# First chunk of an mLSTM cell: gate a spread by TensorE in bfloat16 parts, exponentials four heads at a time, front steps in a new order

## The chip, the cores and the metric

One core of a Trainium2 chip. The time is microseconds on the device for one execution, median of several. The engines are TensorE (PE; its weight loads are listed apart as PEld), VectorE (DVE), ScalarE (ACT), GpSimd (POOL) and SyncE (SP), which here only issues DMAs.

## The reference

Two parts: a recurrent cell with exponential gates over 4 batches x 8 heads, 768 steps, 40 columns a head, then a GELU layer with two weight matrices that arrive in float64.

```python
for t in range(S):
    m_new = np.maximum(f_gate[:, :, t] + m, i_gate[:, :, t])
    f_stab = np.exp(f_gate[:, :, t] + m - m_new)
    i_stab = np.exp(i_gate[:, :, t] - m_new)
    m = m_new
    C = f_stab * C + i_stab * outer(vt, kt)
    n = f_stab * n + i_stab * kt
    h_tilde = C @ qt
    denom = max(abs(n . qt), 1.0)
    y[:, :, t] = sigmoid(o_gate[:, :, t]) * h_tilde / denom
x = y.transpose(0, 2, 1, 3).reshape(B * S, H * D)     # 3072 x 320
h = x @ w_in                                          # 320 x 2048
out = (0.5 * h * (1 + erf(h / sqrt(2)))) @ w_out      # 2048 x 320
```

## The kernel before

The 768 steps are cut into 6 chunks of 128. In a chunk the recurrence becomes products: with bl the running sum of f, a = i - bl and M the running maximum of a, step s contributes to step t with the weight W[s, t] = exp(a[s] - M[t]) for s <= t and 0 beyond. Scores k.q are multiplied by W, and times v (with a column of ones for the denominator) give the new part; the state kept in `state` gives the older one. After the cell of a chunk its 512 tokens (4 batches x 128) go through the up product, GELU and the down product. Work of the next chunk's cell is laced into the down product of the one before.

The order is written by hand: every engine runs its instructions in the order in which the program issues them. `FRONT` is the order for everything up to the down product of chunk 0: a string of words, each a letter with a batch or a count. `play` (L1125) walks it.

- Weights: `P` (`fetch`, L358) starts the DMA of one piece of w_in or w_out as 32-bit words; `K` (`conv_one`, L370) does three VectorE and two ScalarE instructions of its conversion to float32, `J` (`conv_two`, L388) the last two VectorE instructions, and then starts the fetch of the piece four further on (`fetch(i + NB)`; four buffers `bits`). Pieces 0 to 9 are w_in, 10 to 25 w_out. An up step needs pieces 0, 1 and 2, the second 3 and 4 too, and so on; row f of the down product needs piece 10 + f.
- Loads on SP's queue: `L` q and k of a batch, `O` v and o, `B` the M of a later chunk spread over the 128 partitions (512 KB from `M_d`). The batches are counted on over the chunks: `L4` is batch 0 of chunk 1.
- Gates: before the string, `gates_of(0, 1)` makes bl, a and M of chunk 0 on 32 rows (one a head and batch). `E` does chunk 1, `N` chunks 2 to 5, `Q` and `D` turn their decays by TensorE, `d` and `q` spread the last of them (`pd`).
- Cell of chunk 0, in small letters: `w` weights, `g` sigmoid of o, `t` turn k and q (8 transposes into `ps_tr`, copied by ScalarE), `s` scores (two banks of `ps_mm`, tag a, then VectorE's product with W, L550), `c` carry (vw, 8 matmuls, state), `v` values (16 matmuls), `y` finish (6 VectorE instructions), `x` turn y (3 transposes, copied to `first_x`). Cell of chunk 1, in capitals, likewise, with `M` the masking by GpSimd and `R` the split of x.
- `A` and `U` are up steps (L814, L820, then GELU L824) for the first and second half of the tokens, `F` rows of the down product (L1052); rows need all four banks of `ps_mm`. `Z` splits a weight of the next up product.
- Fillers, whose results nobody reads: `k` n runs n matmuls (L228), and `I` n puts n of them (L408) ahead of the next bank's first use.

Weights of chunk 0 (L452): M of that chunk is cut into three bfloat16 parts that add up to it exactly (L307 to L314). For four heads a bank `pm` takes four matmuls that spread the row M of a head over all partitions (the stationary operand is a column of `row`, an identity, repeated 128 times), and one that adds 1e30 where s > t. ScalarE then takes exp(a - pm) head by head, with a, turned to the partitions (`aT`, L315), as bias. In the later chunks M comes by DMA, and the exponentials are head by head too.

Of the kernel before, what the change touches and what calls it, by code (L numbers as in the profile page):

```python
# [9 lines left out]
F32 = mybir.dt.float32  # L10
F32R = mybir.dt.float32r
BF16 = mybir.dt.bfloat16
U32 = mybir.dt.uint32
AF = mybir.ActivationFunctionType
OP = mybir.AluOpType

P = 128
# [8 lines left out]


FRONT = """
    I2 O0 g0 L0 P0 L1 E k1 t0 P1 P2 w0 k7 N k2 w1 O1 K L2 Q s0 O3 w2 q D
    k2 d P3 t1 w3 c0 L3 J v0 t2 K K y0 s1 I7 v1 I8 O2 J g1 L4 I5 c1 K I1  # L30
    I2 y1 s2 x0 t3 B4 O4 B5 g2 J x1 s3 v2 c2 L5 y2 H T0 x2 G0 v3 g3 c3 K y3
    M1 J L6 J A x3 M0 K W0 O7 K A O6 O5 J M2 W1 S0 C0 K J J T1 U U
    K L7 V0 K T2 r J J A G2 K G1 Y0 W2 S1 K M3 C1 A J S2 J K W3 K
    V1 C2 Y1 T3 J J U U S3 V2 K K J G3 J Y2 C3 X0 K V3 J K F J F
    K K B8 F J K F F J K F F F R0 X1 J J K F J F K X2 F J
    K F J Y3 K F R1 e J F Z B9 B10 F X3 R2 Z R3 F p"""
DOWN = """
    M0 F Z F L3 W0 M1 Z W1 S0 C0 F F h0 Q2 F K2 G1 D3 B3 Z V0 G2 M2 W2 M3 W3 V1 K3 Q3 F G0 S2 Z Y0 G3 C2 h2 F
    F Y1 X0 V2 V3 F N F j R0 Y2 Y3 X1 F F X2 R1 F R2 X3 R3 F"""
# [3 lines left out]
def kernel(  # L43
# [16 lines left out]
    nc = tc.nc  # L60

    B, H, S, D = q.shape
    L = P
    NCH = S // L
# [3 lines left out]
    BH = B * H  # L68
# [21 lines left out]
    ps_mm = ctx.enter_context(tc.tile_pool(name="ps_mm", bufs=2, space=bass.MemoryType.PSUM))  # L90
    gp = ctx.enter_context(tc.tile_pool(name="gp", bufs=1))
    gate_ctx = ExitStack()
    gates = gate_ctx.enter_context(tc.tile_pool(name="gates", bufs=1))
# [6 lines left out]
    ident = const.tile([P, P], F32, name="ident")  # L100
# [3 lines left out]
    aT = const.tile([P, NCH, BH], F32, name="aT")  # L104
# [10 lines left out]
    W = {n: shared([P, H, L], F32, f"W{n}") for n in range(B - 1)}  # L115
# [7 lines left out]
    eye = gates.tile([P, P], BF16, name="eye")  # L123
    beyond = gates.tile([P, L], BF16, name="beyond")
# [55 lines left out]
    def load_M(n, to=None):  # L180

        if not B <= n < NCH * B:
            return
        c, b = divmod(n, B)
        src = M_d[c - 1, b * H:(b + 1) * H, :]
        if to is not None:
            Mb[n] = to
            nc.sync.dma_start(out=to, in_=src.unsqueeze(0).to_broadcast([P, H, L]))
            return
        Mb[n] = shared([P, H, L], F32, "W") if n // 2 == NW else wts.tile([P, H, L], F32, name="W", tag="W")  # L190
        nc.sync.dma_start(out=Mb[n].rearrange("p h l -> p (h l)"),
                      in_=src.rearrange("h l -> (h l)").unsqueeze(0).to_broadcast([P, H * L]))
# [17 lines left out]

    keep = gates.tile([BH, NCH, L], F32, name="keep")
    bl = gates.tile([BH, NCH, L], F32, name="bl")
    a = gates.tile([BH, NCH, L], F32, name="a")
    M = gates.tile([BH, NCH, L], F32, name="M")
    ew = gates.tile([BH, NCH - 1, L], F32, name="ew")
    gg = gates.tile([BH, NCH - 1, L], F32, name="gg")
    m0 = gates.tile([BH, NCH], F32, name="m0")
    M_left = gg[:, 0:2]
    M_parts = gates.tile([3 * BH, L], BF16, name="M_parts")
    row = gates.tile([3 * BH, BH], BF16, name="row")  # L220
    for j in range(3):
        m = slice(BH * j, BH * (j + 1))
        nc.scalar.copy(out=row[m], in_=ident[m, m])

    def warm(n):
        cold = ps_h.tile([P, P], F32, name="cold", tag="h")
        for _ in range(n):
            nc.tensor.matmul(cold, w_out[:, 0, 0:P], w_out[:, 0, 0:P], start=True, stop=True, skip_group_check=True)  # L228
# [20 lines left out]
    def gates_turned(*parts):  # L249

        for src, dst in parts:
            n = dst.shape[1]
            pg = ps_tr.tile([P, n, BH], F32, name="pg", tag="tr")
            for c in range(n):
                nc.tensor.transpose(pg[:, c, :], src[:, c, :], ident[0:BH, 0:BH])
            nc.vector.tensor_copy(out=dst, in_=pg)
# [13 lines left out]
    def gates_of(c0, c1):  # L270

        flat = lambda t: t[:, c0:c1].rearrange("p c l -> p (c l)")
        nc.vector.tensor_tensor_scan(out=flat(bl), data0=flat(keep), data1=flat(f_sb), initial=0.0,
                                     op0=OP.mult, op1=OP.add)
        nc.vector.tensor_tensor(out=a[:, c0:c1], in0=i_sb[:, c0:c1], in1=bl[:, c0:c1], op=OP.subtract)
        for c in range(c0, c1):
            nc.vector.tensor_tensor_scan(out=M[:, c], data0=a[:, c], data1=a[:, c], initial=m0[:, c:c + 1],
                                         op0=OP.max, op1=OP.max)
            if c + 1 < NCH:
                nc.vector.tensor_tensor(out=m0[:, c + 1:c + 2], in0=bl[:, c, L - 1:L], in1=M[:, c, L - 1:L],  # L280
                                        op=OP.add)

    def decays_of(e0, e1, g0, g1):

        e, g = slice(e0, e1), slice(g0, g1)
        nc.vector.tensor_tensor(out=ew[:, e], in0=a[:, e], in1=M[:, e, L - 1:L].to_broadcast([BH, e1 - e0, L]),
                                op=OP.subtract)
        nc.vector.tensor_tensor(out=gg[:, g], in0=m0[:, g0 + 1:g1 + 1].unsqueeze(2).to_broadcast([BH, g1 - g0, L]),
                                in1=M[:, g0 + 1:g1 + 1], op=OP.subtract)
        nc.scalar.activation(out=ew[:, e], in_=ew[:, e], func=AF.Exp)  # L290
# [6 lines left out]
    def decays_last(g0, g1):  # L297
        g = slice(g0, g1)
        pd = ps_tr.tile([P, g1 - g0, BH], F32, name="pd", tag="tr")
        nc.tensor.matmul(pd.rearrange("p c n -> p (c n)"), last, gT[:, g].rearrange("p c n -> p (c n)"),  # L300
                         start=True, stop=True)
        by_half = pd.rearrange("p c (n two) -> p c n two", two=2)
        for hip in range(2):
            nc.vector.tensor_copy(out=dec[halves[hip], g], in_=by_half[halves[hip], :, :, hip])


    gates_of(0, 1)  # L307
    left = M[:, 0]
    for j in range(3):
        part = M_parts[BH * j:BH * (j + 1)]  # L310
        nc.vector.tensor_copy(out=part, in_=left)
        if j < 2:
            nc.vector.tensor_tensor(out=M_left[:, j], in0=left, in1=part, op=OP.subtract)
            left = M_left[:, j]  # L314
    gates_turned((a[:, 0:1], aT[:, 0:1]))  # L315
    warm(6)

    def second_gates():
        gates_of(1, 2)
        nc.sync.dma_start(out=M_d[0], in_=M[:, 1])  # L320
        gates_turned((a[:, 1:2], aT[:, 1:2]))
# [84 lines left out]
    def unread(bank):  # L406
        for _ in range(idle[0]):
            nc.tensor.matmul(bank, ident, ident, start=True, stop=True, skip_group_check=True)  # L408
        idle[0] = 0
# [25 lines left out]
    class Cell:  # L435
# [16 lines left out]
        def weights(self, b):  # L452

            n = self.c * B + b
            if self.c > 0:
                W[n] = M_n = Mb.pop(n)
            elif n not in W:
                W[n] = wts.tile([P, H, L], F32, name="W", tag="W")
            for h in range(H):
                r = b * H + h  # L460
                if self.c > 0:
                    src = M_n[:, h, :]
                else:


                    if h % 4 == 0:
                        pm = ps_mm.tile([P, 4, L], F32, name="pm", tag="b")
                        unread(pm[:, 0, :])
                        for j in range(4):
                            nc.tensor.matmul(pm[:, j, :], row[:, r + j:r + j + 1].to_broadcast([3 * BH, P]), M_parts,  # L470
                                             start=(j == 0), stop=False, skip_group_check=True)
                        nc.tensor.matmul(pm, eye, beyond.unsqueeze(1).to_broadcast([P, 4, L]), start=False, stop=True,
                                         skip_group_check=True)
                    src = pm[:, h % 4, :]
                nc.scalar.activation(out=W[n][:, h, :], in_=src, func=AF.Exp, scale=-1.0, bias=aT[:, self.c, r:r + 1])  # L475
            if n in (B, B + 1):
                load_M(n + 2)

# [653 lines left out]
    def in_turn(steps):  # L1132
        todo = list(steps)
        return lambda: todo.pop(0)() if todo else None
# [9 lines left out]
    def first_blocks():  # L1144

        copy_chunk(2, range(1))
        for r in (32, 96):
# [7 lines left out]
                 d=lambda: decays_last(0, 1), q=lambda: decays_last(1, NCH - 1), r=halves_out, p=halves_back,  # L1155
                 A=in_turn(first_up_steps(0)), U=in_turn(first_up_steps(1)), e=first_blocks, F=in_turn(first_down_steps(first_g)),
                 K=in_turn(lambda i=i: conv_one(i) for i in n_pieces), H=products_begin,
                 J=in_turn(lambda i=i: conv_two(i) for i in n_pieces), Z=split_weight)
# [46 lines left out]
```

## Time and profile before

| | us |
|---|---|
| median of 3 runs (462.66 to 463.45) | 463.34 |
| the profiled execution | 463.01 |
| its span, first to last instruction | 461.1 |
| TensorE busy / its weight loads | 453.0 / 402.1 |
| VectorE busy | 337.8 |
| ScalarE busy | 247.3 |
| GpSimd busy | 77.9 |

By group, from the lists of the costliest instructions and of those up to 140 us, with their shapes:

| group | count | busy us | mean ns |
|---|---|---|---|
| L475 exponential, chunk 0, from `pm` 128x128 | 32 | 8.7 | 396 |
| L475 exponential, chunk 1, 128x128 | 32 | 9.8 | 389 |
| L470 matmul 96x128 bf16 into `pm` | 32 | 3.1 | 219 |
| L472 matmul 128x512 bf16 into `pm` | 8 | 3.0 | 381 |
| L814 up matmul of the front 128x256 f32 | 128 | 29.0 | 382 |
| L1052 down matmul of the front 128x320 f32 | 128 | 35.2 | 433 |
| ScalarE table loads up to 140 us | 16 | 20.5 | 1283 |

Busy time of one instruction reaches from its start to its end, and instructions of one engine overlap, so a mean is longer than the distance from one start to the next. A float32 matmul shows as two instructions. The granted clock of TensorE is 0.999 over the run. The profile's lists of waits put idle time down to what ended it; where a wait has several causes the last one is named.

### The profile page before, as it was taken

Reading aid. Unit: us, or ns where it says so; the run is one execution under the profiler, and the core shown is the slowest. Engines: PE = TensorE matmul, PEld = TensorE weight load, DVE = VectorE, ACT = ScalarE, POOL = GpSimd, SP = SyncE. Lnnn points to the kernel's source line nnn. Section 1 sums busy time; section 2 is a strip of 40 time slices with the busy share of each in tenths; the row PEclk is TensorE's granted clock in tenths of the full one; section 3 lists DMA queues with packets and bytes.
Section 4 is the critical chain, followed back from the end, with each engine's and each line's share of the span. In section 5 each row is a group of like instructions: output and inputs, shape, how many; then the busy total and the mean of one; then the engine's idle time right before and its main releaser. Section 6 shows DMA issues by size and latency. Waiting matters only on the chain.

```text
span 461.1 us, 13165 instructions
## 1 busy us (share of the span) xinstructions
PE 453.0 (98%) x5432; PEld 402.1 (87%) x5432; DVE 337.8 (73%) x740; ACT 247.3 (54%) x541; POOL 77.9 (17%) x117
## 2 busy tenths in 40 slices
PE   8999999999999999999999999999999999999996
PEld 8787888877788898998899998899998899988996
DVE  8899879798868988754578754578654577699950
ACT  6986999854454594113494113395113395157701
POOL 3002020000010342300542200542300422100000
PEclk9999999999999999999999999999999999999999
DMA  8997993258967655219955219953018950210001
GB/s 153 206 216 190 211 221 97 73 131 226 157 164 157 117 91 97 66 50 181 161 88 95 66 58 179 156 93 46 4 57 170 166 99 13 80 36 2 1 0 58
DMA packets 174876, 51.12 MB, mean 111 GB/s; under 512 B 154752, under 2 KB 168352, under 8 KB 174816
## 3 DMA queue, kind: packets, MB, share of 16 engines
q1 hardware_dynamic: 174496, 49.95, 53.4%
q8 instruction: 43, 0.70, 0.7%
q10 hardware_dynamic: 320, 0.33, 0.2%
q14 instruction: 17, 0.14, 0.1%
HBM read 45.47 MB, written 10.03 MB: 120 GB/s over the span
## 4 chain that ended last, share of the span: by engine, by line
PE 93%; DVE 3%; DMA 2%; SPq 1%; issue 1%; ACT 0%; DVEq 0%
PE po L1073 26%; PE pu L957 23%; PE po L1052 8%; PE pu L814 6%; PE pu L968 6%; PE po L927 6%; PE ph L665 4%; PE ps L563 3%; PE pu L820 2%; PE px L705 2%; PE pf L618 2%; PE ps L547 1%; SPq L155 1%; PE pf L629 1%; PE cold L228 1%; DMA ob<-in_o_gate_dram 1%
## 5 line engine op out<-in xcount | busy, mean ns | idle before, releaser
L1073 PE MATMUL po<-w_out,g 128*128 128x160 f32 x512 | 74.4, 302 | 0.0
L972 ACT ACTIVATE g<-pu 128x512 f32<-128x512 f32 x64 | 32.2, 620 | 77.4 <-PE pu L968 77.4
L1073 PEld LDWEIGHTS po<-w_out,g 128*128 128x128 f32 x512 | 70.1, 190 | 1.9 <-ACT g L972 1.3
L957 PE MATMUL pu<-x_hi,w_in_hi 128*128 128x512 f32 x160 | 39.0, 387 | 0.0
L475 ACT ACTIVATE W<-W,aT 128x128 f32<-128x128 f32 x128 | 38.7, 388 | 0.1
L957 PE MATMUL pu<-x_lo,w_in_lo 128*128 128x512 f32 x160 | 37.8, 379 | 0.0
L449 POOL TENSOR_SCALAR_AFFINE_SELECT W<-W 128x1024 f32<-128x1024 f32 (+2 forms) x20 | 24.1, 1209 | 80.3 <-DMA W<-M_d 70.0
L1073 PE MATMUL po<-w_sums,sums 128*128 128x160 f32 x256 | 36.9, 302 | 0.0
L1073 PEld LDWEIGHTS po<-w_sums,sums 128*128 128x128 f32 x256 | 35.0, 190 | 0.4
L1052 PE MATMUL po<-w_out,g 128*128 128x320 f32 x128 | 35.2, 433 | 0.0
L957 PEld LDWEIGHTS pu<-x_hi,w_in_hi 128*128 128x128 f32 x160 | 29.5, 189 | 5.7 <-ACT g L972 1.3
L957 PEld LDWEIGHTS pu<-x_lo,w_in_lo 128*128 128x128 f32 x160 | 30.2, 189 | 4.3
L1052 PEld LDWEIGHTS po<-w_out,g 128*128 128x128 f32 x128 | 24.0, 190 | 9.6
L534 POOL TENSOR_TENSOR vw<-vb,ewT 128x328 f32<-128x328 f32 x12 | 8.8, 745 | 136.3 <-DMA vb<-in_v_dram 90.7
L569 DVE TENSOR_TENSOR W<-ps,W 128x256 f32<-128x256 f32 (+1 forms) x48 | 18.1, 416 | 17.0 <-PE ps L563 7.1
L957 PE MATMUL pu<-x_all,w_mid 128*128 128x512 f32 x80 | 30.3, 379 | 0.0
L957 PE MATMUL pu<-x_all,w_in_mid 128*128 128x512 f32 x80 | 30.3, 379 | 0.0
L814 PE MATMUL pu<-first_x,w_in 128*128 128x256 f32 x128 | 29.0, 382 | 0.0
L814 PEld LDWEIGHTS pu<-first_x,w_in 128*128 128x128 f32 x128 | 23.8, 190 | 3.4 <-DVE w_in L396 0.3
L801 DVE TENSOR_TENSOR sums<-g 128x512 f32<-128x512 f32 x16 | 12.3, 770 | 19.6 <-ACT g L972 19.6
L773 DVE TENSOR_TENSOR w_in_mid<-w_in_hi,w_in_lo 128x512 fp32r<-128x512 f32 x20 | 13.7, 685 | 16.5 <-PE pu L957 16.5
L381 ACT ACTIVATE pow<-pow,e_hi 128x320 f32<-128x320 uint32 (+1 forms) x26 | 16.1, 620 | 15.2 <-DVE pow L379 15.2
(199 smaller groups left out, 952.1 us busy)
## 6 DMA issues: line engine op xcount, KB each, us to landing
W<-M_d SPq DMA_DIRECT2D x16, 512.0 KB, 5.3
bits<-in_moe_w_in_dram SPq DMA_DIRECT2D x20, 256.0 KB, 4.3
bits<-in_moe_w_out_dram SPq DMA_DIRECT2D x16, 320.0 KB, 3.2
blocks<-kq_d SPq DMA_DIRECT2D x32, 128.0 KB, 3.2
ob<-in_o_gate_dram SPq DMA_DIRECT2D x24, 160.0 KB, 4.5
out_dram<-o_sb SPq DMA_DIRECT2D x36, 80.0 KB, 2.0
kq_d<-in_k_dram SPq DMA_DIRECT2D x32, 80.0 KB, 2.5
kq_d<-in_q_dram SPq DMA_DIRECT2D x32, 80.0 KB, 2.4
```

What stands on the lines that cost most here:

```text
L381: nc.scalar.activation(out=p, in_=pu, func=AF.Relu, scale=-I23, bias=e_hi)
L449: nc.gpsimd.affine_select(out=x, in_=x, compare_op=OP.is_ge, fill=1.0e30, base=base, pattern=[[0, H], [1, x.shape[2]]], channel_multiplier=-1)
L475: nc.scalar.activation(out=W[n][:, h, :], in_=src, func=AF.Exp, scale=-1.0, bias=aT[:, self.c, r:r + 1])
L569: nc.vector.tensor_tensor(out=w[r, :, t], in0=ps[i][hip][r, :, t], in1=w[r, :, t], op=OP.mult)
L665: nc.tensor.matmul(ph[r, h, :], Pm[:, h, r], vb[turn_of(n)][:, h, :], start=True, stop=True)
L814: nc.tensor.matmul(banks[-1][e][:, i - i0, :], in_tile(i, x)[:, e, i % 2 * P:(i % 2 + 1) * P], first_x[:, x, t0:t1], start=(x == 0 and i = ...
L927: nc.tensor.matmul(in_pairs(po[t]), x[:, t * L:(t + 1) * L], in_turns(w), start=(f, k) == first, stop=(f, k) == last, skip_group_check=True)
L957: nc.tensor.matmul(in_pairs(pus[i][e]), w[k][:, e, i * P:(i + 1) * P], in_turns(x[:, k, :]), start=(n == 0 and k == 0), stop=False, skip_g ...
L968: nc.tensor.matmul(in_pairs(pu[e]), w[r, i // 2, i % 2 * P:(i % 2 + 1) * P], in_turns(x[r, NX, :]), start=False, stop=(n == 2), skip_group ...
L972: nc.scalar.activation(out=g.t[:, HF * e + i, :], in_=pu[e], func=AF.Gelu, scale=4097.0)
L1052: nc.tensor.matmul(po[b], g.t[:, f, b * L:(b + 1) * L], w_out[:, f, :], start=(f == 0), stop=(f == NF - 1))
L1073: nc.tensor.matmul(bank[k][:, t, :], lhs(j, t), rhs(j), start=(first and t == 0 and j == 0), stop=(t == 1 and j == HF - 1), skip_group_che ...
```

## The change

`a` and `M` become the two halves of one tile `aM`, and the three exact bfloat16 parts are made of both at once (`aM_parts`, 256 columns instead of 128). For four heads of chunk 0 one more matmul, with the parts of a as stationary operand and minus the identity's columns, each repeated 128 times, as moving one, puts -a[s] into every column of the bank. The bank then holds M[t] - a[s], and one exponential with scale -1 and no bias does four heads (128x512). The turned `aT` of chunk 0, its transpose and its copy are gone. `row` has a second half with the negated identity, made by one more ScalarE instruction. The string FRONT has the same steps but for fillers, in another order.

```diff
 FRONT = """
-    I2 O0 g0 L0 P0 L1 E k1 t0 P1 P2 w0 k7 N k2 w1 O1 K L2 Q s0 O3 w2 q D
-    k2 d P3 t1 w3 c0 L3 J v0 t2 K K y0 s1 I7 v1 I8 O2 J g1 L4 I5 c1 K I1
-    I2 y1 s2 x0 t3 B4 O4 B5 g2 J x1 s3 v2 c2 L5 y2 H T0 x2 G0 v3 g3 c3 K y3
-    M1 J L6 J A x3 M0 K W0 O7 K A O6 O5 J M2 W1 S0 C0 K J J T1 U U
-    K L7 V0 K T2 r J J A G2 K G1 Y0 W2 S1 K M3 C1 A J S2 J K W3 K
-    V1 C2 Y1 T3 J J U U S3 V2 K K J G3 J Y2 C3 X0 K V3 J K F J F
-    K K B8 F J K F F J K F F F R0 X1 J J K F J F K X2 F J
-    K F J Y3 K F R1 e J F Z B9 B10 F X3 R2 Z R3 F p"""
+    O0 L0 P0 P1 k3 P2 k1 g0 L1 E t0 w0 O1 k6 I1 B4 N O3 w1 K s0 L2 L3 Q w2 q D J w3 t1 c0 v0 K K P3 s1 J t2 y0
+    I9 O2 I4 v1 J I11 L4 g1 c1 K y1 t3 I1 x0 O4 g2 B5 L5 g3 s2 d s3 x1 v2 M1 H c2 y2 T0 x2 G0 v3 c3 K A M0 J
+    y3 x3 J K W0 K A O7 W1 S0 O6 M2 L6 O5 C0 J J K J T1 U U L7 K V0 T2 K W2 M3 J A G2 K J Y0 S1 r C1 A J K S2
+    W3 V1 K C2 J K T3 J G1 U U J K Y1 S3 V2 C3 B8 K J K X0 J J F K J K K J Y2 J R0 G3 K F K F F F F F J F X1
+    V3 F J K e J F K K X2 B9 Y3 F R1 F F B10 J J Z K Z F F X3 R2 J R3 p F"""
@@
-    a = gates.tile([BH, NCH, L], F32, name="a")
-    M = gates.tile([BH, NCH, L], F32, name="M")
+    aM = gates.tile([BH, 2, NCH, L], F32, name="aM")
+    a, M = aM[:, 0], aM[:, 1]
@@
-    M_left = gg[:, 0:2]
-    M_parts = gates.tile([3 * BH, L], BF16, name="M_parts")
-    row = gates.tile([3 * BH, BH], BF16, name="row")
+    aM_left = [gg[:, 0:2], gg[:, 2:4]]
+    aM_parts = gates.tile([3 * BH, 2, L], BF16, name="aM_parts")
+    row = gates.tile([3 * BH, 2, BH], BF16, name="row")
     for j in range(3):
         m = slice(BH * j, BH * (j + 1))
-        nc.scalar.copy(out=row[m], in_=ident[m, m])
+        nc.scalar.copy(out=row[m, 1], in_=ident[m, m])
+    nc.scalar.activation(out=row[:, 0], in_=row[:, 1], func=AF.Copy, scale=-1.0)
@@
-    left = M[:, 0]
+    left = aM[:, :, 0]
     for j in range(3):
-        part = M_parts[BH * j:BH * (j + 1)]
+        part = aM_parts[BH * j:BH * (j + 1)]
         nc.vector.tensor_copy(out=part, in_=left)
         if j < 2:
-            nc.vector.tensor_tensor(out=M_left[:, j], in0=left, in1=part, op=OP.subtract)
-            left = M_left[:, j]
-    gates_turned((a[:, 0:1], aT[:, 0:1]))
+            nc.vector.tensor_tensor(out=aM_left[j], in0=left, in1=part, op=OP.subtract)
+            left = aM_left[j]
     warm(6)
@@
-            for h in range(H):
-                r = b * H + h
-                if self.c > 0:
-                    src = M_n[:, h, :]
-                else:
-                    if h % 4 == 0:
-                        pm = ps_mm.tile([P, 4, L], F32, name="pm", tag="b")
-                        unread(pm[:, 0, :])
-                        for j in range(4):
-                            nc.tensor.matmul(pm[:, j, :], row[:, r + j:r + j + 1].to_broadcast([3 * BH, P]), M_parts,
-                                             start=(j == 0), stop=False, skip_group_check=True)
-                        nc.tensor.matmul(pm, eye, beyond.unsqueeze(1).to_broadcast([P, 4, L]), start=False, stop=True,
-                                         skip_group_check=True)
-                    src = pm[:, h % 4, :]
-                nc.scalar.activation(out=W[n][:, h, :], in_=src, func=AF.Exp, scale=-1.0, bias=aT[:, self.c, r:r + 1])
+            if self.c > 0:
+                for h in range(H):
+                    nc.scalar.activation(out=W[n][:, h, :], in_=M_n[:, h, :], func=AF.Exp, scale=-1.0,
+                                         bias=aT[:, self.c, b * H + h:b * H + h + 1])
+            else:
+                for h in range(0, H, 4):
+                    r = b * H + h
+                    pm = ps_mm.tile([P, 4, L], F32, name="pm", tag="b")
+                    unread(pm[:, 0, :])
+                    nc.tensor.matmul(pm, aM_parts[:, 0], row[:, 0, r:r + 4].unsqueeze(2).to_broadcast([3 * BH, 4, L]), start=True,
+                                     stop=False, skip_group_check=True)
+                    for j in range(4):
+                        nc.tensor.matmul(pm[:, j, :], row[:, 1, r + j:r + j + 1].to_broadcast([3 * BH, P]), aM_parts[:, 1],
+                                         start=False, stop=False, skip_group_check=True)
+                    nc.tensor.matmul(pm, eye, beyond.unsqueeze(1).to_broadcast([P, 4, L]), start=False, stop=True,
+                                     skip_group_check=True)
+                    nc.scalar.activation(out=W[n][:, h:h + 4, :], in_=pm, func=AF.Exp, scale=-1.0)
```

## The prediction

> **What bounds the kernel now.** I read the busy table by stage first, then the chain of waits in order of time, then the timeline of the stretch that the change touches. Columns of the first fence: stretch in us, its length, then busy us (and instructions) of TensorE matmuls, TensorE weight loads, VectorE, ScalarE, GpSimd, then granted clock, DMA share, GB/s.
>
> ```profile
> 10.00:20.00 10.00, 9.28 (x92) 7.61 (x89) 8.32 (x25) 9.00 (x30) 0.00 (x0) 1.00 0.99 186
> 20.00:30.00 10.00, 9.62 (x150) 8.41 (x151) 9.68 (x23) 9.22 (x22) 0.00 (x0) 1.00 1.09 208
> 30.00:40.00 10.00, 9.04 (x154) 7.91 (x150) 9.06 (x24) 6.36 (x15) 0.00 (x0) 1.00 0.93 228
> 50.00:60.00 10.00, 10.00 (x93) 8.97 (x91) 6.23 (x12) 9.91 (x23) 1.09 (x1) 1.00 0.99 216
> 80.00:90.00 10.00, 10.00 (x103) 8.60 (x104) 6.85 (x20) 9.88 (x21) 0.00 (x0) 1.00 0.33 96
> ```
>
> From 40 us on TensorE is full. Before 40 us its busy time contains fillers (cold L228, the ident matmuls of L408); there VectorE (8.3, 9.7, 9.1 of 10) and the DMA engines (share 0.99, 1.09, 0.93) are what is full, and ScalarE has air after 30 us. ScalarE is full only at 50 to 90 us. The chain says when the full stretch begins (start, us, what):
>
> ```profile
> 39.22 1.06 PE ph L665 x32
> 40.28 0.47 PE pf L585 x16
> 40.75 3.65 PE pu L814 x16
> 44.40 1.06 PE pu L820 x8
> 45.46 0.48 PE px L705 x3
> 45.94 3.65 PE pu L814 x16
> ```
>
> From 40.75 to 166.5 us every piece of the chain is TensorE and each starts where the last ends; after that TensorE waits 0.6 us for VectorE once (ps L563). So the end is set by when the first up product (first A, L814) starts, plus the TensorE work behind it, plus any new hole. Both programs have the same TensorE work behind that point: the same turns, products and rows F in slightly other places, x3 and the cell of chunk 1 included. The question is thus when the first A starts, and whether a hole opens later.
>
> **Prices** (timeline of 9 to 40 us; start, us, what; rates are start to start):
>
> ```profile
> 10.56 2.19 ACT L475 ACTIVATE W<-pm,aT 128x128 f32<-128x128 f32 x8
> 45.49 1.08 ACT L824 ACTIVATE g<-pu 128x512 f32<-128x512 f32 x2 [1.30 <-PE pu L820]
> 7.94 0.40 DVE L286 TENSOR_TENSOR ew<-a,M 32x256 f32<-32x256 f32 x1
> 16.98 0.79 SPq L155 DMA_DIRECT2D kb<-in_k_dram  x1
> 38.73 0.49 DVE L534 TENSOR_TENSOR vw<-vb,ewT 128x328 f32<-128x328 f32 x1
> 39.14 0.49 DVE L534 TENSOR_TENSOR vw<-v,ewT 128x328 f32<-128x328 f32 x1
> 48.34 1.28 ACT L475 ACT_TABLE_LOAD   x1
> 49.63 2.45 ACT L475 ACTIVATE W<-W,aT 128x128 f32<-128x128 f32 x8
> ```
>
> VectorE: K on a 512-wide piece 1.39 (14.14 to 15.53), J 1.33 (20.23 to 21.56), a product with W 1.20 (26.16 to 27.36), y 1.70 (24.46 to 26.16), vw 0.41. TensorE: turn 1.02, scores 1.1, values 1.05, carry 0.48, px 0.49, filler 0.25 (14 half-instructions in 1.72).
>
> **Exponentials.** Eight 128x128 of a batch take 2.19 us; two of 128x512 have no row here. Bounds: two gelus of that size from PSUM 1.08 below, 2.19 above (no gain); I take 1.1, the gelu being the same shape and engine. Saved: 4 x 1.1 = 4.4 us of ScalarE, all before 21 us. What it hides in: after the first batch's exponentials (ending 12.75) ScalarE waits until 13.64 for VectorE's ew; from then kT/qT copies come earlier only if TensorE brings the turns earlier. VectorE is the full engine of that stretch, so I price the saving at nothing. Of VectorE's five stalls named below four end with TensorE by the timeline and the fifth carries no name; none ends with ScalarE.
>
> **The spread of a.** Eight matmuls of 128x512 bf16. The row nearest is the eye matmul of the same shape, 10.07 to 10.29: 0.22 each, 1.76 us, bounds 0.2 to 0.38 (its latency). One transpose (0.24) and the copy aT for chunk 0 (0.19) go. It stands where TensorE runs fillers: 28 before, 27 after. Without that cover it costs 1.5 us; I take 0 and let it delay the W's where the walk below says so.
>
> **The splits** are twice as wide: three casts of 0.21 to 0.22 (32x128) become 32x256, between 0 and 0.13 more each (the second by a cast costing like L288 to L286, 0.27 to 0.40); two subtracts +0.13. Sum 0.3 to 0.65, less the aT copy: 0.36 us on VectorE. But the later gates wait for something later still: the transpose of chunk 1's a stands behind the fillers k3 k1 plus the fixed six, 10 where 7 stood after a transpose: at 8.1 instead of 7.54. ew begins at 8.5 instead of 7.94, and everything to the end of the gates (14.14) moves to 14.7: +0.55.
>
> **The new order, walked from there.** VectorE: K 16.1, product s0 17.3, ewT/gT 17.75, dec after pd 18.66, ewT and gT 19.15, J 20.5, vw0 20.9, two K 23.7, product s1 (scores end 23.95) 25.2, J 26.55, y0 28.25, J 29.6, vw1 30.0, K 31.4, y1 33.1. TensorE: w3 ends 20.3, t1 21.3, c0, v0 22.85, s1 23.95, t2 25, v1 27.1, 11 fillers 29.8, c1 30.5, t3, x0, s2 33.4. Product s2 33.45 to 34.65. s3 needs s2's banks (ps_mm has two of tag a, scores take both): 34.65 to 35.75, its product 35.8 to 37.0. From there to the first A the two programs have the same steps (vw2, y2, two vw, T0, x2, v3, c3): 36.6 to 40.68 before, 4.05 us, so A at 41.1. Here VectorE does the same work as before in the stretch (4 K, 3 J, 4 products, 3 y, 5 vw: 21.6 us plus the small copies) with the same 2.0 us of stalls (before 0.58, 0.18, 0.59, 0.17, 0.49; after 0.45, 0.1, 0.3, 0.35, 0.8). That is +0.4 us with every transfer in time.
>
> **Transfers.** P1 and P2 (1 MB) move ahead of L1 on SP's queue, and B4 (512 KB, M for chunk 1) moves from the 31.52 us place to right behind O1, with the M_d write that it must wait for. Behind it queue O3, L2, L3, P3, O2. Cumulative KB ahead of and with kb of batch 2: 3408 before (issued 16.98, landed 4.6 later, 21.6), 4240 after. From vb's landing at 18.4 to kb's at 35.2 the queue brought 3296 KB: 196 KB/us. From bits at 10.5 the later 2896 KB land at 25.3; counting a small-packet 160 KB load at 1.0 us and a 512 KB piece at 2.0 (spacing of the landings: k2 21.6, v3 22.5; k3 27.4 to v2 30.1), at 24.0. t2 wants it at 23.95: 0 to 1.35 us of hole on TensorE, and the 11 fillers then end after vw1 instead of before. The same count for piece 3 (used by K at 30.0) gives 30 to 31.5, for kb of T0 (wanted at about 38.4) 38 to 40.6. I take +0.6 us from these; the bounds are 0 and 2.5. First A at 41.7, +1.0.
>
> **Behind the first A.** ScalarE loads its tables 17 times up to the sigmoid of the last chunk-1 batch, 15 before; both extra loads fall at 66 to 93 us, where it is full. 2 x 1.28 = 2.57 us. Before, the first gelus of the last U free bank a at 89.6 and row F0 starts at 92.86: 3.2 us of slack. After, 2.57 goes to tables and 0.75 because v of batch 3 (V3) moved behind F7: slack about -0.1. The sigmoid of batch 1 stands just before these gelus, and y1, the product s3 and the bank that X0 wants queue behind it on VectorE: same margin. I take 0.2 us; bounds 0 and 1.5. Rows F have their w_out pieces 1.5 us or more ahead in my count, as before (124.8 against 126.3 for the last).
>
> [...]
>
> **Sum:** 0.4 + 0.6 + 0.2 = +1.2 us. On the profiled execution: span 461.1 to 462.3, with the 1.9 us outside it (463.01 - 461.1) 464.2; the median of the runs stands 0.33 above that execution: 464.5 us.
>
> **Rivals.**
> - *Transfers and tables stay hidden* (+0.4, 463.7). For it: the queue is never empty up to there, and the W broadcast may cost less than its bytes (between kb at 35.2 and ob at 38.5 it and two loads took 3.3 us). Against: DMA share 0.99 to 1.09 just there.
> - *ScalarE becomes the bound at F0* (+1.2 and 1.5 more: 466.0). For it: 9.9 of 10 busy at 50 to 90 us and two more loads. Against: the walk leaves it at zero, not below.
> - *Faster:* VectorE's 2.0 us of stalls at 16 to 36 us vanish because W, kT and qT are ready ahead, the freed 4.4 us of ScalarE being what TensorE's turns and scores waited for. Then A starts at 41.1 - 2.0 = 39.1, -1.6 us: 461.7. It decides if the s3 product starts before 35.4, its place now. For it: ps L547 waits 0.43 us for qT at 34.23. Against: that wait is outside the stretch in which ScalarE is relieved, and s3 now waits for a bank.
> - *The change does not do what it says:* no sign; the eight wide exponentials are in the program.
>
> **How the numbers follow.** A measurement here tells 0.2%, 0.93 us, from no change. Forecast 0.40 (own range 463.6 to 465.6; 0.06 of it within 0.2%), hidden 0.30, ScalarE bound 0.15, faster 0.15 (0.02 of it within 0.2%). Faster 0.13, same 0.30 + 0.06 + 0.02 = 0.38, slower 0.34 + 0.15 = 0.49. The range 462.4 to 466.6 leaves out most of the faster case and the far end of the transfers (2.5).
>
> **What would show it.** ew (L286) at 8.5; two exponentials of a batch in 1.1; turns of batch 2 at 24 to 25.3 after a DMA wait; s3 scores released by VectorE; L814 first at 41 to 42.7 (below 40 the faster case is right); row F0 2 to 2.5 us behind the last chunk-1 product; the same TensorE chain after. It is wrong if VectorE is not full at 15 to 37, or if TensorE shows holes between the first A and F0.

## The result, and the profile after

The changed kernel takes 469.3 us (median of 6 runs, 468.67 to 472.29), the kernel before 463.36 us on the same chip (6 runs, 462.66 to 464.36): 1.0143 times as long, 95% interval 1.0124 to 1.0162. The forecast was 464.5 us with a range of 462.4 to 466.6. The direction was right, the size was not. The profiled execution of the changed kernel took 468.99 us, its span is 467.2 us, 6.1 us more than before.

Lines of the changed file lie about 3 lower than those of the file before: the up product L814 is L811 now, the turn L525 is L522, the exponentials of chunk 0 stand on L472. The table by stage of the changed kernel, with the columns of the first table of the prediction:

```profile
10.00:20.00 10.00, 9.33 (x88) 6.87 (x87) 8.88 (x25) 6.08 (x12) 0.00 (x0) 1.00 1.09 201
20.00:30.00 10.00, 7.78 (x107) 7.10 (x104) 9.51 (x21) 7.92 (x14) 0.00 (x0) 0.83 0.99 225
30.00:40.00 10.00, 9.49 (x128) 8.35 (x126) 5.55 (x15) 4.80 (x11) 0.00 (x0) 1.00 1.03 223
```

ScalarE did get its time back: 6.08 us busy of 10 to 20 where it had 9.00. But from 20 to 30 us TensorE is busy for 7.78 us (before 9.62) and its mean granted clock is 0.83 (before 1.00), and from 30 to 40 us VectorE falls from 9.06 to 5.55. The engine that was full is now waiting for something. The chain of waits in order of time (start, us, what) says for what:

```profile
21.26 4.72 DMA kb<-in_k_dram
...
26.11 1.76 PE pt L522 x8
27.88 1.71 PE ph L405 x8
29.58 1.15 PE ph L662 x32
30.73 2.65 PE pf L405 x22
...
42.52 1.80 DVE vw L531 x2
...
45.13 3.65 PE pu L811 x16
```

The k of batch 2 is issued at 21.26 (before 16.98) and lands at 25.98, and only then can its turn run. TensorE stood idle for 2.22 us ahead of it. The turn takes 1.76 us in the place of 1.02, eight filler instructions take 1.71 in the place of 0.98 (reckoned from the 14 in 1.72 of the prediction), and the first up product (the first A) starts at 45.13 in the place of 40.75. The table of the same execution in stretches of 1 us shows why the turn is slow (the third number from the end is the granted clock):

```profile
25.00:26.00 1.00, 0.00 (x0) 0.00 (x0) 0.96 (x3) 0.44 (x1) 0.00 (x0) 1.00 0.90 141
26.00:27.00 1.00, 0.89 (x5) 0.92 (x6) 1.00 (x3) 0.00 (x0) 0.00 (x0) 0.66 1.18 226
27.00:28.00 1.00, 1.00 (x7) 1.00 (x6) 0.87 (x4) 0.68 (x2) 0.00 (x0) 0.50 0.98 315
28.00:29.00 1.00, 1.00 (x7) 1.00 (x7) 0.95 (x3) 0.98 (x2) 0.00 (x0) 0.50 0.99 326
29.00:30.00 1.00, 1.00 (x17) 0.78 (x16) 0.98 (x2) 0.99 (x2) 0.00 (x0) 0.63 1.05 397
30.00:31.00 1.00, 1.00 (x29) 0.95 (x26) 0.05 (x1) 0.28 (x1) 0.00 (x0) 1.00 1.05 379
```

TensorE's idle time (24 to 26, no instruction) is followed by a clock of half speed. In stretches of 0.02 us the clock is 1.00 up to 26.32, 0.50 from 26.34 to 29.72 and 1.00 again from 29.74: 3.4 us at half speed, just when the late turn is on the path. The kernel before has 1.00 in all these stretches.

Why k is late is seen on SP's queue (start, us of the issuing instruction with its wait):

```profile
10.60 3.54 SPq L317 DMA_DIRECT2D M_d<-aM  x1
...
17.11 0.34 SPq L188 DMA_DIRECT2D W<-M_d  x1
```

The same queue in the kernel before:

```profile
8.07 2.20 SPq L320 DMA_DIRECT2D M_d<-M  x1
```

The list of waits on the queue of the changed kernel has for B4 (us in total, times, longest):

```profile
SPq L188 <- DMA M_d<-aM: 1.8, 1, 1.8
```

The write of M_d, behind six weight fetches where two stood before, holds the queue for 3.54 us (before 2.20). Its data were not what it waited for: the list of waits puts these 3.5 us down to VectorE, but VectorE had finished that M at 7.54. By the queue's timelines the hold is 3.23 (e4) to 4.59 us (e5) with six fetches ahead and 1.83 (e8) to 2.20 (the kernel before) with two. The broadcast W<-M_d (step B4), which needs what M_d wrote, waits another 1.8 us and is issued only at 17.11. The loads of batch 2 come behind it. The transfer of k itself is no slower: 4.7 us from its issue to its landing, against 4.6 before and 4.5 and 5.3 in the runs e5 and e7 below. What moved is its issue.

A smaller wait stands just ahead of the first A. The carry of batch 3 waits 0.39 us for its vw, which VectorE makes while GpSimd masks W. GpSimd's timeline of the changed kernel, then VectorE's:

```profile
42.86 2.41 POOL L446 TENSOR_SCALAR_AFFINE_SELECT W<-W 128x1024 f32<-128x1024 f32 x2 [38.49 <-DMA W<-M_d]
```

```profile
42.93 1.39 DVE L531 TENSOR_TENSOR vw<-v,ewT 128x328 f32<-128x328 f32 x1
```

The same vw took 0.49 us before, where the masking began at 41.13, behind it.

After the first A the distance grows from 4.4 us to 5.8 at the end of the rows F (134.32 against 128.50). One step of it, first ScalarE's timeline of the changed kernel (start, us, what):

```profile
77.27 1.28 ACT L821 ACT_TABLE_LOAD   x1
...
79.67 1.28 ACT L478 ACT_TABLE_LOAD   x1
...
82.50 1.28 ACT L821 ACT_TABLE_LOAD   x1
```

TensorE's timeline of the same execution at the last U (the bracket is idle time and what ended it):

```profile
85.19 7.17 PE L811 MATMUL pu<-first_x,w_in 128*128 128x256 f32 x32 [0.93 <-DVE W L547]
```

ScalarE switches from gelu to sigmoid and back within 6 us for one sigmoid of batch 1. The power step behind it (the two ScalarE instructions of a weight's conversion, K) is late, VectorE's J waits 3.21 us for it, the product with W stands behind J, and TensorE waits for that product: a hole of 0.93 us in a stretch where it had none.

### The profile page after: what moved, and what is told of

Same layout as the page of the kernel before. It is cut to its first block, busy times and chain, and to the rows that moved or that the text cites. A ratio compares the mean times of both kernels' runs of the same rounds, so it can differ in the third digit from the quotient of the medians.

```text
span 467.2 us, 13160 instructions
## 1 busy us (share of the span) xinstructions
PE 455.5 (98%) x5437; PEld 403.8 (86%) x5437; DVE 339.6 (73%) x739; ACT 246.7 (53%) x520; POOL 79.2 (17%) x117
## 4 chain that ended last, share of the span: by engine, by line
PE 75%; DVE 12%; ACT 9%; issue 3%; DMA 1%; SPq 1%; DVEq 0%
PE po L1070 24%; PE pu L954 22%; PE pu L965 6%; PE po L924 6%; PE ph L662 3%; PE ps L560 2%; PE pu L811 2%; ACT W L458 2%; DVE w_out L393 1%; PE pf L615 1%; PE px L702 1%; DVE pow L390 1%; ACT pow L378 1%; ACT g L821 1%; PE cold L226 1%
## 5 line engine op out<-in xcount | busy, mean ns | idle before, releaser
L811 PE MATMUL pu<-first_x,w_in 128*128 128x256 f32 x128 | 29.2, 382 | 1.2 <-DVE W L547 0.9
L811 PEld LDWEIGHTS pu<-first_x,w_in 128*128 128x128 f32 x128 | 23.8, 190 | 4.9 <-DVE W L547 1.2
```

What stands on the lines that cost most here:

```text
L811: nc.tensor.matmul(banks[-1][e][:, i - i0, :], in_tile(i, x)[:, e, i % 2 * P:(i % 2 + 1) * P], first_x[:, x, t0:t1], start=(x == 0 and i = ...
```

## The experiments

Two theories stood at the start. H: the new order, not the new computation, makes the kernel slower; B4 too early on SP's queue makes k of batch 2 late, TensorE's hole costs itself and then half the clock. C: the computation (spread of a on TensorE, wide splits) costs the time. First A and last U are given by TensorE's timeline, which shows the first A before at 40.68 and the last U at 79.80. FRONT is the string that holds the order.

**e1 and e2: the computation alone, the order alone.**

```diff
 e1: the changed kernel with
-FRONT = (the new order)
+FRONT = (the order before)
 e2: the kernel before with
-FRONT = (the order before)
+FRONT = (the new order)
```

> The new spread of a and the wide exponentials with the old order of the front. Theory H (the new order delays k of batch 2, TensorE stands idle 2.2 us, its clock is halved for 4 us and the fillers then lie on the path): the computation alone is nearly free, 463.3 to 464.5 us, first up product at 40.7 to 41.7. Rival C (the computation itself costs: the extra matmuls, the wider splits): 466 us or more.

> The old computation (exponentials head by head, a as bias) with the new order. H: as slow as the changed kernel or slower, 469 to 471.5 us, hole at the turn of batch 2 and a granted clock near 0.5 behind it. Rival C: back near 463 to 465 us.

The kernel before took 463.72 us (13 runs) in this group. e1: 463.39 us, ratio 0.9996 (0.9986 to 1.0005), first A at 41.14. e2: 469.41 us, ratio 1.0123 (1.0108 to 1.0138), first A at 44.10. The order is the whole loss; what the computation costs or brings is too small for these runs to tell from zero. C falls. (In e2 the order meets the slow exponentials too: TensorE has five small holes of 0.32 to 0.65 us between 15 and 20 us, three of them over when the clock falls; the clock is at one half from 18.4 to 25.2 us, and no hole is left ahead of the turn of batch 2. So e2 shows that the order costs the time, but not through the same hole.)

**e3: B4 four loads later.**

```diff
 the changed kernel, FRONT:
-... k6 I1 B4 N O3 ... I1 x0 O4 g2 B5 ...
+... k6 I1 N O3 ... I1 x0 B4 O4 g2 B5 ...
```

> The changed kernel with one word moved: B4 (M of chunk 1 spread over the partitions, 512 KB) from behind O1 to ahead of O4, as before. H: k of batch 2 lands 1.5 to 2 us earlier than 26.0, the hole is under 0.7 us, the granted clock stays at 1.0, the first up product starts at 41.5 to 43 instead of 45.1, time 465 to 467 us. Rival (the transfer is not what holds the turn): within 0.7 us of 469.3.

465.95 us, ratio 1.0055 (1.0040 to 1.0070): 3.4 of the 5.9 us are gone by moving one transfer. k of batch 2 was issued at 20.00, and TensorE's timeline shows a short hole, and the later one unchanged:

```profile
25.05 0.63 PE L522 MATMUL pt<-ident,kb 128*128 128x128 f32 x4 [0.55 <-DMA kb<-in_k_dram]
...
81.90 7.17 PE L811 MATMUL pu<-first_x,w_in 128*128 128x256 f32 x32 [0.93 <-DVE W L547]
```

The clock was 1.00 from 24 to 30 us. First A at 41.81.

**e4: fillers in the hole.**

```diff
 the changed kernel, FRONT:
-... s1 J t2 y0 I9 ...
+... s1 J I9 t2 y0 I9 ...
```

> The changed kernel with 9 fillers ahead of the turn of batch 2, in the hole. Transfers stay as they are. H with the clock as a part of it: the granted clock stays at 1.0 through 26 to 30 us, the turn takes 1.0 instead of 1.76 us and the next fillers 1.0 instead of 1.7, so 1.3 to 1.6 us less than the changed kernel: 467.6 to 468.1. Rival (only the wait counts, the clock is a side effect): 469.3 or more, since fillers add work.

467.57 us (465.94 to 467.99), ratio 1.0081 (1.0058 to 1.0103). k came no earlier, the turn started at 26.38 instead of 26.11, but it ran at full clock, the eight fillers took 1.06 us where the timeline shows 1.92 without the edit, and the first A came at 43.10 (45.06 in the changed kernel). Of these 1.96 us 1.36 are there when the 22 fillers start (29.30 in the place of 30.66), and 0.39 is the wait for vw, which this run does not have. The half clock is thus worth about 1.4 us by the timeline; the medians differ by 1.7.

**e12: two moves alone.** Not a part undone but a part done: the old order with the early fetches P1 P2 and the early B4, and nothing else.

```diff
 e1 (new computation, order before), FRONT:
-... P0 L1 E k1 t0 P1 P2 w0 k7 N ... t3 B4 O4 B5 ...
+... P0 P1 P2 L1 E k1 t0 w0 k7 B4 N ... t3 O4 B5 ...
```

> e1_compute_only (new computation, old order) with two moves of the new order alone: the weight fetches P1 P2 next to P0, ahead of the loads of batch 1, and the first broadcast of M (B4) ahead of the later gates. Theory H (these two make M_d wait in SP's queue, B4 wait for M_d's landing, and the loads of batch 2 wait behind B4): k of batch 2 issued near 20.5 in the place of 17.36 and landed near 25.3, a hole of 1 to 2 us ahead of its turn (due at 23.75), a granted clock under 0.8 for some us behind it, first A 43 to 44, median 466.5 (465.5 to 467.5). Rival (it takes the whole of the new order): median under 464.5.

466.8 us (465.39 to 467.06; ratio 1.0065, 1.0046 to 1.0084), 3.4 us over e1. SP's queue in e12:

```profile
16.95 0.34 SPq L191 DMA_DIRECT2D W<-M_d  x1
...
21.25 0.63 SPq L155 DMA_DIRECT2D kb<-in_k_dram  x1
```

TensorE's timeline in e12, at the turn of batch 2:

```profile
25.98 1.08 PE L525 MATMUL pt<-ident,kb 128*128 128x128 f32 x4 [2.37 <-DMA kb<-in_k_dram]
```

The queue, the hole and the clock (0.50 from 26 to 29 us) are those of the changed kernel; the first A came at 44.68, somewhat later than expected. One of the four executions had a mean clock of 1.000 and took 465.39 us, the three others 0.995 or 0.996 and 466.77 to 467.06. So these two moves are enough for the main loss, and e3 shows that B4 is needed for it.

**e7 and e13: the table loads.**

```diff
 e7: e3, e13: the changed kernel; both, FRONT:
-... T2 K W2 M3 J A G2 K J Y0 S1 ... T3 J G1 U U ...
+... T2 K M3 J A G2 K G1 J Y0 W2 S1 ... T3 J U U ...
```

> e3_b4_late with G1 moved beside G2 and W2 moved behind Y0, as in the kernel before: two table loads fewer on ScalarE between 70 and 92 us. Theory S (e3's loss after its first A, 1.1 us late, grows to 2.1 at the last U because ScalarE's extra loads of 1.28 us make S2's product late): TensorE's hole ahead of the last U is gone, last U near 80.9 in the place of 81.90, median 465.0 (464.5 to 465.4), against e3's 465.95. Rival (the loads only move work inside a stretch that another engine bounds): 465.7 to 466.2.

> The changed kernel with G1 beside G2 and W2 behind Y0, as in the kernel before, and nothing else: two table loads fewer on ScalarE. In e7 this edit was worth 1.9 us on top of the later B4. Theory S (the loads' loss adds to that of the late k, it does not lie behind it): median 467.4 (466.8 to 468.0). Rival (the two losses overlap, so that with the late k the loads are hidden): 468.8 to 469.6.

e7 took 464.05 us (10 runs), ratio 1.0010 (0.9999 to 1.0022), 1.9 us under e3 and no longer to be told from the kernel before. By the medians the two table loads are worth twice what was expected. TensorE's timeline in e7 has a short hole ahead of the turn and none ahead of the last U:

```profile
24.49 0.63 PE L522 MATMUL pt<-ident,kb 128*128 128x128 f32 x4 [0.73 <-DMA kb<-in_k_dram]
...
80.62 7.07 PE L811 MATMUL pu<-first_x,w_in 128*128 128x256 f32 x32
```

In the profiles the last U moved by 1.28 us, of which 0.22 was there at the first A already, and the end of the rows F by 1.61 (130.98 to 129.37). The profiled execution of e7 is one of its slowest, 465.25 us; what it lost behind the rows is told under e8. On the changed kernel itself (e13) the same edit gave 468.79 us (466.8 to 469.57; ratio 1.0108, 1.0084 to 1.0131): 0.5 us, near the rival's number. The profiled execution went from the first A to the first row F in 50.6 us where the changed kernel took 52.4, but its first A came 1.7 us later, at 46.72: the turn of batch 2 0.8 us later, behind a hole of 2.56 us, and the last carry another 0.9, as it waited 1.28 us for vw where the changed kernel waited 0.39. So the edit shortens the later stretch; how much of it reaches the end is not settled, as these two waits differ from one execution to the next by more than the effect.

**e5 and e11: fewer fillers.** In the changed kernel 22 filler instructions ran from 30.73 to 33.38 ahead of a carry whose vw was ready at 29.9.

```diff
 e5: the changed kernel, FRONT:
-... v1 J I11 L4 g1 c1 ...
+... v1 J I1 L4 g1 c1 ...
 e11: e4, FRONT:
-... v1 J I11 L4 g1 c1 ...
+... v1 J I4 L4 g1 c1 ...
```

> The changed kernel with I1 in the place of I11 behind J (1 filler step in the place of 11 ahead of the carry of batch 1). In the changed kernel these fillers ran from 30.73 to 33.38 while vw of batch 1 was ready at 29.9. Theory H (late TensorE makes fillers that covered a wait a part of the path): the carry starts near 31.0, first A near 42.8 in the place of 45.13, median 467.0 (466.3 to 467.8). Rival (the fillers only fill a wait on VectorE's chain that ends at the same time): first A stays near 45, median 469.0 to 469.6.

> e4_fill_hole (9 filler steps ahead of the late turn of batch 2, clock at 1.00) with I4 in the place of I11 ahead of the carry of batch 1. In e4 vw of batch 1 was ready at 30.41 and the fillers ended at 31.95. Theory H (fillers behind a late turn are a part of the path): the carry starts near 30.5, first A near 41.7 in the place of 43.10, median 466.2 (465.6 to 466.8). Rival (weights of J and the bits' transfers end the stretch at the same time): 467.2 to 467.9. This takes up e5_short_fill, where a transfer that came 1.4 us later hid the answer.

Both failed. e5: 470.4 us (469.23 to 471.34; ratio 1.0143, 1.0120 to 1.0167), no better than the changed kernel. In its profile k landed later still, the hole was 3.66 us, and the clock stood at one half from 26.3 to 33.1 us; all four executions had a mean clock of 0.993. The first A came at 44.59. e11: 469.35 us (466.62 to 470.58; ratio 1.0135, 1.0113 to 1.0157), no faster than e4's 467.57. Its profiled execution (mean clock 1.000, 466.62 us) had the first A 0.69 us earlier than e4's, half of what was expected; the three others had mean clocks of 0.992 to 0.996 and took 468.76 to 470.58 us. Taking out fillers that lie on the path by the profile brought nothing: most of these executions have the lower clocks. Whether it is the fewer fillers that lower the clock was not tried by itself and stays open.

**e8: the fetches P1 P2 later, and the fillers k3 between them left out.**

```diff
 e7, FRONT:
-O0 L0 P0 P1 k3 P2 k1 g0 L1 E t0 w0 ...
+O0 L0 P0 k1 g0 L1 E t0 P1 P2 w0 ...
```

> e7 with the two weight fetches P1 P2 behind the second gates and the first mask's turn, as in the kernel before, and without the warm step k3 ahead of them. Theory Q (the six early weight fetches fill SP's queue: M_d waits 3.5 us in it instead of 1.7, and k of batch 2 is issued 2.6 us later than with before's order; the warm steps delay the transposed a by 0.9): k of batch 2 lands before 24.0, no hole ahead of its turn, first A near 41.2 (e3: 41.88), median 464.3 (463.7 to 464.8). Rival (VectorE's chain and not the transfers sets first A): no change against e7.

465.05 us, ratio 1.0034 (1.0021 to 1.0048): 1.0 us slower than e7, which neither theory had. Q fell. M_d's hold on the queue did shrink from 4.06 to 1.83 us, but the second M_d write then held it for 2.94 us in the place of 0.81, and k of batch 2 was issued at 18.96 in the place of 19.09. The wait had moved, not gone. Nor does the front show the lost 1.0 us: by the profiles the first A came at 41.56 (e7 41.59), and the rows F ended at 129.17 (129.37). What e8's profiled execution has behind them is a hole of 1.73 us on TensorE ahead of the carry at 179.53 (L626), for which the profile names no cause; e7's has one of 1.38 us there, the kernel before 0.29, e1 and e3 none. Whether most executions of e8 have it, and why, stays open.

**e9 and e10: can the freed ScalarE time be used?** In e1 VectorE still sets the front, so its small copies go to ScalarE.

```diff
 e9: e1 with
-            nc.vector.tensor_copy(out=dst, in_=pg)
+            nc.scalar.copy(out=dst, in_=pg)
 (the same for dec), FRONT:
-... q D k2 d ... I5 c1 ...
+... q D d ... I1 c1 ...
 e10: e9, FRONT:
-... t3 B4 O4 B5 g2 ... H T0 x2 G0 ...
+... t3 O4 g2 ... H T0 B4 B5 x2 G0 ...
```

> e1_compute_only (new computation, old order) with the seven copies of transposed gates and decays on ScalarE instead of VectorE (1.8 us of VectorE before the first carry) and with 2 and 4 filler steps left out (k2 ahead of d, I5 to I1 ahead of c1). Theory V (VectorE bounds the front, so the 4.4 us that the wide exponentials free on ScalarE are worth something only if VectorE's work goes there): first A near 40.3 in the place of 41.21, median 462.4 (461.8 to 462.9). Rival (TensorE's own order and ScalarE's queue bound it; the copies wait there behind exponentials): 463.4 to 464.5.

> e9 with the two broadcasts of M for chunk 1 (B4 B5) moved behind the fourth turn of chunk 1's first batch (T0), so that GpSimd's two masking selects no longer run from 41.5 to 43.9. Theory G (in e9 VectorE's y_rest and J steps took 0.99 and 1.59 us in the place of 0.23 and 0.69 while GpSimd's select ran, 1.7 us in all, and this made the two holes of 0.24 and 0.56 on TensorE behind the first A): these two instructions take 0.23 and 0.69 again, the holes are gone or at most 0.2, median 462.8 (462.3 to 463.3). Rival (the next wait ends at the same time: the selects meet the next J steps, or the table switch of the chunk-1 exponentials sets the pace): 463.4 to 464.2.

e9: first A at 39.76, 1.4 us earlier than e1, yet 463.62 us, ratio 1.0007 (0.9996 to 1.0018). 0.80 us went at once: two holes (0.24 and 0.56) where TensorE waited for weights from VectorE. There VectorE ran slowly while GpSimd masked W (41.51 to 43.85), by VectorE's timeline in e9:

```profile
41.89 0.99 DVE L693 COPY y_rest<-ob 128x128 f32<-128x128 f32 x1
42.80 1.59 DVE L392 SCALAR_TENSOR_TENSOR pow<-bits,pow 128x512 uint32<-128x512 uint32 x1
```

e10 moves the transfer that the masking waits for, so the masking runs from 44.38 to 46.84. VectorE's timeline in e10:

```profile
41.77 0.23 DVE L693 COPY y_rest<-ob 128x128 f32<-128x128 f32 x1
41.92 0.68 DVE L392 SCALAR_TENSOR_TENSOR pow<-bits,pow 128x512 uint32<-128x512 uint32 x1
...
44.57 1.31 DVE L378 TENSOR_SCALAR pow<-bits 128x512 uint32<-128x512 uint32 x1
```

The same two instructions take 0.23 and 0.68, both holes are gone, and the stretching has moved to two later ones (0.42 to 1.31 each) which nobody waits for. The first row F starts at 92.05 (before 92.79), the lead at chunk 1's up products is 0.74 us (127.76 against 128.50), and it melts at later chunks: 0.40 us at 198, 0.11 at 337. The time is 463.31 us (12 runs), ratio 0.9998 (0.9986 to 1.0011). The mechanism is shown, a gain is not. No version here beats the kernel before.

**The account.** 469.3 (changed) to 465.95 (B4 later) to 464.05 (two table loads fewer) to 463.39 (the rest of the order as before): 3.35 + 1.9 + 0.66 us. These are medians of three groups of runs; against the kernel before of its own group each is 5.9, 2.2, 0.4 and -0.3 us off, which makes the steps 3.7, 1.8 and 0.7. They hold for this order of undoing: the table loads taken out first (e13) gave 0.5. In e7 the first row F starts at 92.77, as before, but the values of batch 3 (0.75 us) are still to come and run between the rows, which end at 129.37 against 128.50; that fits the last 0.66, but was not tried by itself.

## Why the prediction was wrong, step by step

- *The small prices were right.* ew began at 8.34 (forecast 8.5), a wide pair of exponentials took 1.05 or 1.06 us twice and 1.26 twice (1.1; so 4.1 us were saved, 4.4 forecast), a spread matmul 0.22 (0.22), the gates ended at 14.6 (14.7). "I price the saving at nothing" held too: e1 is 0.9996 of before.
- *The walk with transfers in time (+0.4)* fits: it put the product with scores s1 at 23.95, the trace has it at 23.93; and e7, with the transfers nearly in time, has its first A at 41.59, of which 0.73 is a hole still left.
- *The step that failed is the term for transfers,* "I take +0.6 us from these; the bounds are 0 and 2.5". It had the right place: "t2 wants it at 23.95: 0 to 1.35 us of hole on TensorE". But k landed at 25.98 and not from 24.0 to 25.3. The landings were counted by bytes and by the spacing of earlier ones; the prediction names "the M_d write that it must wait for" and gives that wait no time, and the queue stood for it 1.8 us behind a write that had itself held it for 3.54. The hole came to 2.16 us against 23.95, still inside the bounds. But the sum had no term for the clock behind a hole: 0.74 on the turn, 0.73 on the fillers, 0.10 on the values, 1.57 us together, and that is outside. Against the walk's 41.1 the first A came 3.96 us late by the timeline; hole and clock are 3.73 of it, and the wait of batch 3's carry for a vw stretched beside GpSimd's masking, 0.39, covers the remaining 0.23. The term measured 3.7 us in the place of 0.6.
- *The term for ScalarE's tables (+0.2, bounds 0 and 1.5)* was too small: 1.9 us by the medians of e3 and e7, 1.1 up to the last U by their profiles, though only 0.5 by the medians on the changed kernel itself (e13). The path was named, "the product s3 and the bank that X0 wants queue behind it on VectorE", but for the stretch ahead of the first row F; it struck 12 us earlier, ahead of the last U, through J and the product of batch 2.
- *The rivals.* "Transfers and tables stay hidden" failed on both counts. "ScalarE becomes the bound" was right as a mechanism, and it came on top of the late transfer, not instead of it; the cases were priced as if only one could come. "Faster" failed: scores were not what the freed ScalarE time brought forward; VectorE and the queue stood in the way.
- *The range* took in 2.5 us of late transfer and 1.5 of ScalarE one at a time, but not both, nor the clock. (The prediction says that it leaves out the far end of the transfers; by its own sum, 0.4 + 2.5 + 0.2, that end is 466.4 us and lies inside.)

## What to carry to other kernels

A transfer that depends on another transfer did not only cost its bytes on SP's queue here: B4 stood 1.8 us for the landing of M_d, and what was queued behind it stood with it (with B4 later, in e7, k of batch 2 was issued at 19.09 in the place of 21.26). So walk the queue by issue times and not by kilobytes. Price a hole on TensorE with the clock behind it, here about 1.6 us on top of 2.2, and add up risks that can come together. Where an engine is relieved, look at which engine bounds that stretch; a saving elsewhere (4.1 us of ScalarE here) brought nothing by itself (e1: 0.9996 of before), and when work of the bound was moved to it, the lead of 0.74 us melted to 0.11 in later chunks (e10).

## What the runs showed of the hardware

- A hole of 2.22 us (2.37 in e12) on TensorE was followed by about 3.4 us at half clock, one of 3.66 us (e5) went with 6.8 us at half clock, from 26.3, still in the hole, to 33.1; holes of 0.55 to 1.31 us ahead of the same turn (e3, e7, e8) were followed by none. By the mean clocks the same program had it in some executions and not in others (e12: 0.995 or 0.996 in three, 1.000 in one). In e2 the clock fell without a long hole, behind three of 0.32 to 0.57 us within 2.3 us, and stayed at one half for 6.8 us.
- While GpSimd's masking select ran, some VectorE instructions took two to four times as long: a copy 0.99 for 0.23 us, a scalar_tensor_tensor 1.59 for 0.68, a tensor_scalar 1.31 for 0.42, and in the changed kernel a tensor_tensor 1.39 for 0.49; e10 moved the overlap and the stretching went with it.
- k of batch 2 landed between 25.98 and 27.4 us in executions (the changed kernel, e5) that issue the same transfers in the same order up to there; its issue moved (21.26 and 22.89), its transfer took 4.7 and 4.5.
- The issue of one small write (M_d, 16 KB) was held for 3.23 (e4) to 4.59 us (e5) behind six weight fetches of 256 KB, for 1.83 (e8) to 2.20 (the kernel before) behind two.
